# Loads of q, k and v queued behind attention's transposes, and the router's two halves side by side, in an attention, MoE, MoE kernel

## The chip, the cores and the metric

One Trainium2 chip, of which one core is used. The metric is the device time of one execution in microseconds (us). The time before is the median of three runs.

## What is computed

Causal attention with a decay, then a dense feed-forward layer with a squared ReLU ("MoE1"), then a layer of eight experts of which each token uses two ("MoE2"), all in fp32 as the reference has it:

```python
# q, k, v: (4, 8, 576, 64), f: (4, 8, 576)
cum = np.cumsum(np.log(np.clip(f, 0.0001, 1.0)), axis=-1)
scores = q @ k.T / 8 + (cum[:, :, :, None] - cum[:, :, None, :])   # causal
x = softmax(scores) @ v                        # -> (2304, 512)
h = np.maximum(x @ w_in, 0.0)                  # (2304, 2048)
x = h * h @ w_out                              # (2304, 512)
logits = x @ w_gate + np.log1p(np.exp(x @ w_noise)) * noise    # (2304, 8)
# top two experts by softmax of their logits; out = sum of gate * (relu(x @ w1[e]) @ w2[e])
```

## The kernel before

**Precision.** The matmuls run on fp16 pairs: a high part and a low remainder of each operand, and three products (high x high, high x low, low x high; the list `HL3`). So each fp32 product is three fp16 products that are summed in PSUM.

**Attention.** The four batches have 576 queries each. The first 256 of each ("head") are done in a part of their own, of 12 sub-units (`subs`); the first eight of them, and the first eight feed-forward blocks of chunk 0, follow an order written out by hand (`PLAN`, L58). The rest is 48 units `(b, i, p)`: batch, block of 128 queries (i = 2, 3, 4; the last has 64), pair of heads. A unit goes through four steps, one "tick" apart (`att_tick`, L971): scores and exponentials (`att_s`, `att_exp`), the split into high and low parts and a DMA transpose on SP's queue into `pt` (`att_split`, L280; the transposes are at L291 for i = 2, 3 and at L302 for i = 4), and, three ticks after the split, the product with the values (`att_pv`, L330 and L333). The head's last sub-units have the same transpose at L516 and the product at L529. Here such a transpose into `pt` is called a turn.

**Operands of a unit.** For each batch and pair, q and k are loaded by `load_qk` (L110, 896 KB, two buffers `qkr`), and made into high and low parts by `prep` (ScalarE L207, L208, DVE L209, L210, a small DMA L213 on POOL's queue). v is loaded by `load_v` (L104, 320 KB, two buffers `vr`) and split by `prep_v` (ScalarE L220, DVE L221). In a tick with i = 4, batch b + 1 is prepared for pair p, and the load of its next pair is written right behind that; loads of v stand in the ticks with i = 4 and i = 2.

**MoE1.** The 2304 tokens are six chunks of 384; the hidden 2048 are 16 blocks. A step of the main loop (from L1120) does the first layer of one block (`mm1`, L599, 12 matmuls of 384 columns, then ReLU and square on ScalarE, L606 to L610) and the second layer of the block two steps before (`mm2`, L655, nine matmuls of 512 columns). Chunks 0 and 1 are done in two passes each of eight blocks. The ticks of attention are spread over the steps by `target` (L1145): `until` says which tick a pass has to reach. The third pass (n = 2: chunk 0, blocks 8 to 15) has the first seven ticks. The weights of a block are loaded by `load_w` (L555, 1 MB): the first eight on SP's queue, the others on POOL's, and converted by `conv_w`.

**Router and MoE2.** When a chunk is done, `x2_out` scales it, splits it and turns it (`x2T`), and a few steps later `router` computes 8 + 8 columns of logits for its three tiles of 128 tokens (L742, 36 matmuls per chunk: three tiles, four parts of the 512, three products of 16 columns), then the top two and, in `slots`, each token's place in its experts' tables. MoE2 gathers the rows of an expert and runs its two layers (L931, L948).

**What sets the order.** Behind the hand-written part (from L1102), a scheduler orders the instructions of each engine: by their place in the program, and by when a simulated machine finds them ready. DMAs are issued in the order of the queue of the engine that issues them (SP, or POOL). `tc.issue_after(x)` orders by hand: what its block traces on the same engine as x comes behind x on that engine; instructions of other engines are not tied, and nothing waits for x to finish. The dictionary `pin` holds the instructions so used. `pin["sp"]` is set at L1088 and by the head's turns at L516, and used by `load_v` and `load_qk` (L103, L109); `pin["pool"]` is the last load of weights on POOL's queue.

Of the kernel before, what the change touches and what calls it, by code (L numbers as in the profile page):

```python
# [37 lines left out]
NT = CH // 128  # L38
# [34 lines left out]
def attn_moe_moe_kernel(ctx: ExitStack, tc, qka, qk, v, fr, w_io, wgn, noise, w1, w2, out):  # L73
# [206 lines left out]
    def att_split(u):  # L280
        b, i, p = u
        pr, = st[u]
        if i < 4:
            phl = astream.tile([128, 4, 2, 2, 128], F16, name="phl", bufs=3)
            pt = astream.tile([128, 4, 2, 2, 128], F16, name="pt", bufs=3)
            for h in range(2):
                pv = pr[:, h, :128 * (i + 1)].rearrange("p (k s) -> p k s", s=128)
                hi, lo = phl[:, :i + 1, h, 0, :], phl[:, :i + 1, h, 1, :]
                nc.scalar.activation(hi, pv, AF.Copy)  # L289
                nc.vector.tensor_tensor(lo, pv, hi, op=ALU.subtract)  # L290
            nc.sync.dma_start_transpose(out=pt[:, :i + 1].rearrange("p a b c q -> p (a b c) q"),  # L291
                                        in_=phl[:, :i + 1].rearrange("p a b c s -> p (a b c s)"))
        else:
            pt = astream.tile([128, 5, 2, 128], F16, name="pt", bufs=3)
            ph4 = astream.tile([128, 5, 2, 128], F16, name="ph4", tag="phl", bufs=3)
            nc.gpsimd.memset(ph4[:, 4, :, 64:128], 0.0)
            flat = pr.rearrange("p z s -> p (z s)")
            for k0, k1, w_ in ((0, 4, 128), (4, 5, 64)):
                s3 = flat[:, 128 * k0:128 * k0 + w_ * (k1 - k0)].rearrange("p (k s) -> p k s", s=w_)
                nc.scalar.activation(ph4[:, k0:k1, 0, :w_], s3, AF.Copy)  # L300
                nc.vector.tensor_tensor(ph4[:, k0:k1, 1, :w_], s3, ph4[:, k0:k1, 0, :w_], op=ALU.subtract)
            nc.sync.dma_start_transpose(out=pt.rearrange("p a b q -> p (a b) q"),  # L302
                                        in_=ph4.rearrange("p a b s -> p (a b s)"))
        st[u] = [pt]

    po_t = {}
# [425 lines left out]
    def router(c, pool=(psS, "S", 3, 512), behind=None):  # L732
        rt = gpool
        pl = pool[0].tile([128, pool[3]], F32, name="pl", tag=pool[1], bufs=pool[2])
        for t in range(NT):
            x = 0
            for cc in range(4):
                for wi, xi in HL3:
                    with ExitStack() as guard:
                        if behind is not None:  # L740
                            guard.enter_context(tc.issue_after(behind))
                        nc.tensor.matmul(pl[:, 16 * t:16 * t + 16], x2T_t[t][:, 4 * xi + cc, :], wg[:, cc, wi, :],  # L742
                                         start=(x == 0), stop=(x == 11))
                    x += 1
        lg = rt.tile([128, NT, 16], F32, name="lg", bufs=1)
        nc.vector.tensor_scalar(lg, pl[:, :16 * NT].rearrange("p (t e) -> p t e", t=NT), 2.0 ** -17, None, op0=ALU.mult)
        e_ = rt.tile([128, NT, NE], F32, name="e_", bufs=1)
        u_ = rt.tile([128, NT, NE], F32, name="u_", bufs=1)
        l_ = rt.tile([128, NT, NE], F32, name="l_", bufs=1)
        nc.scalar.activation(e_, lg[:, :, 8:16], AF.Exp)  # L750
        nc.vector.tensor_scalar(u_, e_, 1.0, None, op0=ALU.add)
        nc.scalar.activation(l_, u_, AF.Ln)
        d_ = rt.tile([128, NT, NE], F32, name="d_", bufs=1)
        nc.vector.tensor_scalar(d_, u_, -1.0, None, op0=ALU.add)
        nc.vector.tensor_sub(e_, e_, d_)
        nc.vector.reciprocal(u_, u_)
        nc.vector.tensor_mul(e_, e_, u_)
        nc.vector.tensor_add(l_, l_, e_)
        nc.vector.tensor_mul(l_, l_, nz[:, NT * c:NT * c + NT, :])
        nl = rt.tile([128, NT, NE], F32, name="nl", bufs=1)  # L760
        nc.vector.tensor_add(nl, l_, lg[:, :, 0:8])
        m8 = rt.tile([128, NT, 8], F32, name="m8", bufs=1)
        i8 = rt.tile([128, NT, 8], U32, name="i8", bufs=1)
        for t in range(NT):
            nc.vector.max(m8[:, t, :], nl[:, t, :])
            nc.vector.max_index(i8[:, t, :], m8[:, t, :], nl[:, t, :])
        idf = rt.tile([128, NT, 2], F32, name="idf", bufs=1)
        nc.vector.tensor_copy(idf, i8[:, :, 0:2])
        ent = rt.tile([128, NT, 2, 2], I32, name="ent", bufs=3)
        gv = ent.bitcast(F32)  # L770
        dd = rt.tile([128, NT], F32, name="dd", bufs=1)
        ed = rt.tile([128, NT], F32, name="ed", bufs=1)
        nc.vector.tensor_sub(dd, m8[:, :, 1], m8[:, :, 0])
        nc.scalar.activation(ed, dd, AF.Exp)
        nc.vector.tensor_scalar(dd, ed, 1.0, 1.0e-9, op0=ALU.add, op1=ALU.add)
        nc.vector.reciprocal(gv[:, :, 0, 1], dd)
        nc.vector.tensor_mul(gv[:, :, 1, 1], ed, gv[:, :, 0, 1])
        for t in range(NT):
            nc.vector.tensor_scalar(ent[:, t, :, 0], pid.to_broadcast([128, 2]), SPARE + CH * c + 128 * t, None, op0=ALU.add)
        oh = rt.tile([128, NT, 2, NE], F32, name="oh", bufs=1)  # L780
        for t in range(NT):
            for k in range(2):
                nc.vector.tensor_scalar(oh[:, t, k, :], iota8, idf[:, t, k:k + 1], None, op0=ALU.is_equal)
        m_ = rt.tile([128, NT, NE], F16, name="m_", bufs=1)
        nc.vector.tensor_add(m_, oh[:, :, 0, :], oh[:, :, 1, :])
        for t in range(NT):
            j = NT * c + t
            nc.vector.tensor_add(mprev[:, j + 1, :], mprev[:, j, :], m_[:, t, :])
        return m_, oh, ent
# [181 lines left out]
    def att_tick(k, pool_of):  # L971
# [12 lines left out]
        if k < NU:  # L984
# [6 lines left out]
            b, i, p = u  # L991
            if i == 4 and b + 1 < B:
                prep(b + 1, p)
                if p < 3:
                    load_qk(b + 1, p + 1)
                elif b + 2 < B:
                    load_qk(b + 2, 0)
                if p > 1:
                    load_v(b + 1, p - 2)
            if i == NB and b:  # L1000
                prep_v(b, p)
                if p < 2:
                    load_v(b, p + 2)
        if k % 4 == 1:
            x_copies(k)
        if 0 <= k - 1 < NU:
            att_split(units[k - 1])

    turn = [0]

# [109 lines left out]
    for s_i, (n, c, i) in enumerate(steps):  # L1120
# [21 lines left out]
            slots(c - 1, router(c - 1, bank), bank)  # L1142
        a0, a1 = ([-3] + until)[n] + 3, until[n] + 3
        i0, i1 = passes[n][1:]
        target = a0 + (a1 - a0) * (i - i0 + 1) // (i1 - i0)  # L1145
        j = s_i - NA + NPL
        if NPL <= j < NSUB + 3:
            hd_tick(j, main_bank)
# [15 lines left out]
        for w_i in new:  # L1164
            with tc.issue_after(pin["prev"]):
                conv_w(w_i)
            if w_i + 2 < NF:
                with tc.issue_after(pin["pool"]):
                    pin["pool"] = load_w(w_i + 2, nc.gpsimd).ins
        if c in (2, 3) and i % 4 == 3:  # L1170
            zero_out(4 * (c - 2) + i // 4)
# [169 lines left out]
```

## Time and profile before

| | us |
|---|---|
| median of 3 runs | 959.05 |
| lowest, highest | 950.98, 960.93 |
| the profiled execution, its own time | 958.06 |
| its span, first to last instruction | 956.1 |
| PE busy in the span | 929.3 |
| DVE, ScalarE (ACT), POOL busy | 567.7, 447.3, 205.1 |

The profile is of one execution. PE is TensorE's matmul, PEld its weight load, SPq the queue of SyncE, on which most DMAs are issued; times within it count from the span's start. A DMA's row in a timeline shows how long its issue took, not its transfer; the time to its landing is told apart. In brackets behind a row stand the engine's idle time ahead of it and what ended it. Matmuls overlap, so a group's span is what counts, not the sum of their durations.

### The profile page before, as it was taken

Reading aid. Unit: us, or ns where it says so; the run is one execution under the profiler, and the core shown is the slowest. Engines: PE = TensorE matmul, PEld = TensorE weight load, DVE = VectorE, ACT = ScalarE, POOL = GpSimd, SP = SyncE. Lnnn points to the kernel's source line nnn. Section 1 sums busy time; section 2 is a strip of 40 time slices with the busy share of each in tenths; the row PEclk is TensorE's granted clock in tenths of the full one; section 3 lists DMA queues with packets and bytes.
Section 4 is the critical chain, followed back from the end, with each engine's and each line's share of the span. In section 5 each row is a group of like instructions: output and inputs, shape, how many; then the busy total and the mean of one; then the engine's idle time right before and its main releaser. Section 6 shows DMA issues by size and latency. Waiting matters only on the chain.

```text
span 956.1 us, 17598 instructions
## 1 busy us (share of the span) xinstructions
PE 929.3 (97%) x6859; PEld 540.5 (57%) x6859; DVE 567.7 (59%) x1254; ACT 447.3 (47%) x990; POOL 205.1 (21%) x247
## 2 busy tenths in 40 slices
PE   9899989998999999999999999999999999999995
PEld 6675545554555555555555444656574747565652
DVE  7987968877878778776364552545261525343220
ACT  6776679866567567755343421424050504132110
POOL 5000030022121032011024135342414141211102
PEclk9899999999999999999999999999999999999998
DMA  9566799969789858936168946696968594841203
GB/s 341 172 186 193 189 283 269 165 184 199 174 187 227 192 139 204 170 57 110 29 206 218 223 115 122 146 249 181 192 147 202 141 202 114 172 98 21 35 12 44
DMA packets 220871, 155.60 MB, mean 163 GB/s; under 512 B 176690, under 2 KB 187314, under 8 KB 218738
## 3 DMA queue, kind: packets, MB, share of 16 engines
q1 hardware_dynamic: 208370, 125.14, 53.8%
q0 software_dynamic: 12416, 29.31, 15.1%
q8 instruction: 55, 0.90, 0.4%
q14 instruction: 30, 0.25, 0.1%
HBM read 89.05 MB, written 23.98 MB: 118 GB/s over the span
## 4 chain that ended last, share of the span: by engine, by line
PE 82%; DMA 7%; issue 4%; DVE 3%; ACT 2%; POOL 0%; SPq 0%; POOLq 0%; DVEq 0%; ACTq 0%
PE e L948 21%; PE e L931 20%; PE acc L655 16%; PE m L599 13%; PE m1s L599 3%; PE po L330 2%; DMA w<-in_w_io_dram 2%; DMA pt<-phl 1%; DMA qkr<-in_qk_dram 1%; PE ps L237 1%; PE po L472 1%; PE ps L238 1%; PE po L333 1%; DMA pt<-ph 1%; PE ps L248 1%
## 5 line engine op out<-in xcount | busy, mean ns | idle before, releaser
L948 PE MATMUL e<-w2s,hT 128*128 128x512 f16 (+1 forms) x960 | 209.3, 379 | 0.8 <-DVE hT L936 0.8
L655 PE MATMUL acc<-w,g 128*128 128x512 f16 x864 | 205.6, 379 | 0.0
L931 PE MATMUL e<-xgT,w1s 128*128 128x310 f16 (+2 forms) x1536 | 204.7, 294 | 0.0
L931 PEld LDWEIGHTS <-w1s 128*128 128x128 f16 x1536 | 139.6, 97 | 63.9
L599 PE MATMUL m<-xT,w 128*128 128x384 f16 x960 | 172.5, 328 | 2.1 <-ACT r L606 1.6
L935 ACT ACTIVATE hT<-e 128x310 f16<-128x310 f32 (+2 forms) x128 | 54.4, 429 | 251.7 <-PE e L931 251.4
L948 PEld LDWEIGHTS <-hT 128*128 128x128 f16 (+1 forms) x960 | 99.5, 104 | 107.4 <-DVE hT L936 1.3
L599 PEld LDWEIGHTS <-w 128*128 128x128 f16 x1152 | 108.8, 98 | 76.5 <-issue 5.3
L655 PEld LDWEIGHTS <-g 128*128 128x128 f16 x864 | 81.3, 98 | 87.5 <-issue 0.9
L951 DVE TENSOR_SCALAR y<-e,gs 128x512 f32<-128x512 f32 (+1 forms) x40 | 30.0, 750 | 151.6 <-PE e L948 141.7
L936 DVE SCALAR_TENSOR_TENSOR hT<-e,hT 128x310 f16<-128x310 f32 (+2 forms) x128 | 60.5, 477 | 65.0 <-ACT hT L935 64.8
L952 POOL DMA_INDIRECT out_dram<-y,tix x40 | 65.1, 1627 | 141.9 <-DVE y L951 135.0
L813 POOL DMA_INDIRECT table<-ent,si x36 | 42.0, 1167 | 133.8 <-DVE si L810 77.5
L889 POOL DMA_INDIRECT xg<-x2d,tix x40 | 42.4, 1059 | 125.2 <-DMA xgT<-xg 117.8
L266 DVE TENSOR_REDUCE sm<-ps 128x1 f32<-128x384 f32 (+2 forms) x96 | 52.9, 562 | 25.6 <-PE ps L239 12.3
L606 ACT ACTIVATE r<-m 128x384 f32<-128x384 f32 x80 | 39.1, 488 | 52.2 <-PE m L599 52.1
L616 DVE TENSOR_TENSOR r<-r 128x384 f32<-128x384 f32 x64 | 35.3, 552 | 35.4 <-ACT g L607 35.3
L269 ACT ACTIVATE pr<-ps,sm 128x384 f32<-128x384 f32 (+1 forms) x64 | 40.2, 630 | 30.0 <-DVE sm L268 22.5
L607 ACT ACTIVATE g<-r 128x384 f16<-128x384 f32 x96 | 50.2, 523 | 3.3 <-PE acc L655 1.3
L854 DVE SCALAR_TENSOR_TENSOR w2s<-wr,w2s 128x1024 f16<-128x1024 f32 x32 | 39.1, 1222 | 19.6 <-ACT w2s L853 19.5
L853 ACT ACTIVATE w2s<-wr 128x1024 f16<-128x1024 f32 x32 | 33.7, 1052 | 30.8 <-DMA wr<-in_w_dram 30.1
L290 DVE TENSOR_TENSOR phl<-pr,phl 128x384 f16<-128x384 f32 (+1 forms) x64 | 39.0, 619 | 12.8 <-ACT phl L289 12.3
(282 smaller groups left out, 1071.7 us busy)
## 6 DMA issues: line engine op xcount, KB each, us to landing
wr<-in_w_dram SPq DMA_DIRECT2D x64, 512.0 KB, 4.7
qkr<-in_qk_dram SPq DMA_DIRECT2D x16, 896.0 KB, 5.5
w<-in_w_io_dram SPq DMA_DIRECT2D x8, 1024.0 KB, 5.6
w<-in_w_io_dram POOLq DMA_DIRECT2D x8, 1024.0 KB, 5.5
vr<-in_v_dram SPq DMA_DIRECT2D x16, 320.0 KB, 4.0
x2d<-x SPq DMA_DIRECT2D x18, 256.0 KB, 2.7
hraw<-in_qka_dram SPq DMA_DIRECT2D x8, 512.0 KB, 8.9
out_dram<-zero SPq DMA_DIRECT2D x5, 768.0 KB, 4.2
```

The costliest lines, as they stand in the source:

```text
L266: seen[u] = nc.vector.tensor_reduce(sm[:, z:z + 1], ps[z][:, :N], AX.X, ALU.max).ins
L269: nc.scalar.activation(pr[:, z, :N], ps[z][:, :N], AF.Exp, bias=sm[:, 2 + z:3 + z], scale=SC_S, accum_out=su[:, p // 2, z, p % 2:p % 2 + 1])
L599: nc.tensor.matmul(ps, W[i][:, wi, 0, 128 * cc:128 * cc + 128], xT[:, xi, cc, r0:r0 + CH], start=(x == 0), stop=(x == 11))
L607: nc.scalar.activation(g[:, 0, :], r, AF.Square, scale=2.0 ** -10)
L655: last[0] = nc.tensor.matmul(acc[t], g[:, gi, 128 * t:128 * t + 128], W[i][:, wi, 1, :], start=(i in ends[c][0] and x == 0), stop=(i in en ...
L813: s_ = nc.gpsimd.indirect_dma_start(out=table, out_offset=bass.IndirectOffsetOnAxis(ap=si[:, t, k:k + 1], axis=0), in_=ent[:, t, k, :], in ...
L889: nc.gpsimd.indirect_dma_start(out=xg, out_offset=None, in_=x2d[0:seen, :], in_offset=bass.IndirectOffsetOnAxis(ap=rows_t[key, j][0], axis=0))
L931: last[0] = nc.tensor.matmul(ps[:, :hw], w1s[:, cc, wi, 128 * i:128 * i + 128], xgT[:, 4 * xi + cc, c], start=(x == 0), stop=(x == 11)).ins
L935: relu[0] = nc.scalar.activation(hi, ps[:, :hw], AF.Relu).ins
L936: nc.vector.scalar_tensor_tensor(hT[:, i, 1, c], ps[:, :hw], 0.0, hi, op0=ALU.max, op1=ALU.subtract)
L948: last[0] = nc.tensor.matmul(ps[:m], hT[:, i, hi, 128 * j:128 * j + m], w2s[:, i, wi, :], start=(i == 0 and x == 0), stop=(i == NFE - 1 an ...
L952: s_ = nc.gpsimd.indirect_dma_start(out=out, out_offset=bass.IndirectOffsetOnAxis(ap=ix[:m], axis=0), in_=y[:m], in_offset=None, compute_o ...
```

## The change

Four edits, in five places. (1) `att_split` stores its transpose as `pin["sp"]`, so that each later load of q, k or v is issued behind the latest turn traced before it; and in `att_tick` the loads in the ticks with i = 4 and i = 2 are traced after the tick's `att_split` and not before it. (2) The loads of MoE1's weights on POOL's queue are put under `issue_after(pin["sp"])` too. (3) The router multiplies the high part of x by the high and low parts of the weights in one matmul of 32 columns, and the low part by the high part in one of 16; the two halves of the 32 columns are added behind the matmuls by one more DVE instruction. (4) In the third pass the ticks are one step later; in the other passes `target` is as it was.

```diff
--- before.py
+++ after.py
@@ -288,8 +288,8 @@
                 hi, lo = phl[:, :i + 1, h, 0, :], phl[:, :i + 1, h, 1, :]
                 nc.scalar.activation(hi, pv, AF.Copy)
                 nc.vector.tensor_tensor(lo, pv, hi, op=ALU.subtract)
-            nc.sync.dma_start_transpose(out=pt[:, :i + 1].rearrange("p a b c q -> p (a b c) q"),
-                                        in_=phl[:, :i + 1].rearrange("p a b c s -> p (a b c s)"))
+            pin["sp"] = nc.sync.dma_start_transpose(out=pt[:, :i + 1].rearrange("p a b c q -> p (a b c) q"),
+                                                    in_=phl[:, :i + 1].rearrange("p a b c s -> p (a b c s)")).ins
         else:
             pt = astream.tile([128, 5, 2, 128], F16, name="pt", bufs=3)
             ph4 = astream.tile([128, 5, 2, 128], F16, name="ph4", tag="phl", bufs=3)
@@ -299,8 +299,8 @@
                 s3 = flat[:, 128 * k0:128 * k0 + w_ * (k1 - k0)].rearrange("p (k s) -> p k s", s=w_)
                 nc.scalar.activation(ph4[:, k0:k1, 0, :w_], s3, AF.Copy)
                 nc.vector.tensor_tensor(ph4[:, k0:k1, 1, :w_], s3, ph4[:, k0:k1, 0, :w_], op=ALU.subtract)
-            nc.sync.dma_start_transpose(out=pt.rearrange("p a b q -> p (a b) q"),
-                                        in_=ph4.rearrange("p a b s -> p (a b s)"))
+            pin["sp"] = nc.sync.dma_start_transpose(out=pt.rearrange("p a b q -> p (a b) q"),
+                                                    in_=ph4.rearrange("p a b s -> p (a b s)")).ins
         st[u] = [pt]
 
     po_t = {}
@@ -735,15 +735,19 @@
         for t in range(NT):
             x = 0
             for cc in range(4):
-                for wi, xi in HL3:
+                for xi in range(2):
+                    w_ = 32 >> xi
                     with ExitStack() as guard:
                         if behind is not None:
                             guard.enter_context(tc.issue_after(behind))
-                        nc.tensor.matmul(pl[:, 16 * t:16 * t + 16], x2T_t[t][:, 4 * xi + cc, :], wg[:, cc, wi, :],
-                                         start=(x == 0), stop=(x == 11))
+                        nc.tensor.matmul(pl[:, 32 * t:32 * t + w_], x2T_t[t][:, 4 * xi + cc, :],
+                                         wg[:, cc].rearrange("p a b -> p (a b)")[:, :w_],
+                                         start=(x == 0), stop=(x == 7), skip_group_check=True)
                     x += 1
         lg = rt.tile([128, NT, 16], F32, name="lg", bufs=1)
-        nc.vector.tensor_scalar(lg, pl[:, :16 * NT].rearrange("p (t e) -> p t e", t=NT), 2.0 ** -17, None, op0=ALU.mult)
+        p2 = pl[:, :32 * NT].rearrange("p (t a e) -> p t a e", t=NT, a=2)
+        nc.vector.tensor_scalar(lg, p2[:, :, 0, :], 2.0 ** -17, None, op0=ALU.mult)
+        nc.vector.scalar_tensor_tensor(lg, p2[:, :, 1, :], 2.0 ** -17, lg, op0=ALU.mult, op1=ALU.add)
         e_ = rt.tile([128, NT, NE], F32, name="e_", bufs=1)
         u_ = rt.tile([128, NT, NE], F32, name="u_", bufs=1)
         l_ = rt.tile([128, NT, NE], F32, name="l_", bufs=1)
@@ -991,20 +995,22 @@
             b, i, p = u
             if i == 4 and b + 1 < B:
                 prep(b + 1, p)
+            if i == NB and b:
+                prep_v(b, p)
+        if k % 4 == 1:
+            x_copies(k)
+        if 0 <= k - 1 < NU:
+            att_split(units[k - 1])
+        if k < NU:
+            if i == 4 and b + 1 < B:
                 if p < 3:
                     load_qk(b + 1, p + 1)
                 elif b + 2 < B:
                     load_qk(b + 2, 0)
                 if p > 1:
                     load_v(b + 1, p - 2)
-            if i == NB and b:
-                prep_v(b, p)
-                if p < 2:
-                    load_v(b, p + 2)
-        if k % 4 == 1:
-            x_copies(k)
-        if 0 <= k - 1 < NU:
-            att_split(units[k - 1])
+            if i == NB and b and p < 2:
+                load_v(b, p + 2)
 
     turn = [0]
 
@@ -1142,7 +1148,7 @@
             slots(c - 1, router(c - 1, bank), bank)
         a0, a1 = ([-3] + until)[n] + 3, until[n] + 3
         i0, i1 = passes[n][1:]
-        target = a0 + (a1 - a0) * (i - i0 + 1) // (i1 - i0)
+        target = a0 + (a1 - a0) * (i - i0 + (n != 2)) // (i1 - i0)
         j = s_i - NA + NPL
         if NPL <= j < NSUB + 3:
             hd_tick(j, main_bank)
@@ -1165,7 +1171,7 @@
             with tc.issue_after(pin["prev"]):
                 conv_w(w_i)
             if w_i + 2 < NF:
-                with tc.issue_after(pin["pool"]):
+                with tc.issue_after(pin["pool"]), tc.issue_after(pin["sp"]):
                     pin["pool"] = load_w(w_i + 2, nc.gpsimd).ins
         if c in (2, 3) and i % 4 == 3:
             zero_out(4 * (c - 2) + i // 4)
```

## Rows read from the trace of the kernel before

**Rows 1.** The page: busy us per engine (share, instructions), and the granted clock in 40 slices.

```profile
PE 929.3 (97%) x6859; PEld 540.5 (57%) x6859; DVE 567.7 (59%) x1254; ACT 447.3 (47%) x990; POOL 205.1 (21%) x247
...
PEclk9899999999999999999999999999999999999998
```

**Rows 2.** PE's waits over the span: who waited for what, us in total, times, longest.

```profile
PE po L333 <- DMA pt<-ph: 3.0, 1, 3.0
PE po L330 <- DMA pt<-phl: 2.1, 2, 1.2
PE po L529 <- DMA pt<-phl: 2.0, 2, 1.6
...
PE m L599 <- ACT r L606: 1.6, 4, 0.6
PE ps L237 <- DVE setk L209: 1.3, 1, 1.3
```

**Rows 3.** Timeline of PE, last chunk's router: start us, length us, line, tiles, count.

```profile
549.90 1.05 PE L742 MATMUL pl<-wg,x2T 128*128 128x16 f16 x36
550.80 5.34 PE L931 MATMUL e<-xgT,w1s 128*128 128x512 f16 x24
```

**Rows 4.** Timeline of SP's queue and PE, 157 to 166 us, around unit 1's turn.

```profile
157.99 0.57 SPq L104 DMA_DIRECT2D vr<-in_v_dram  x1
...
158.66 2.40 SPq L291 DMA_TRANSPOSE pt<-phl  x1
...
164.61 0.41 PE L330 MATMUL po<-vs,pt 128*128 128x64 f16 x8 [0.88 <-DMA pt<-phl]
```

**Rows 5.** Tile `pl`, its reader: duration ns min/median/max, first and last start.

```profile
L746 DVE TENSOR_SCALAR lg<-pl x6: 198/204/208, 197.1 to 551.3; 128x48 f32<-128x48 f32 x6
```

**Rows 6.** Timeline of SP's queue, 209 to 216 us.

```profile
210.38 0.33 SPq L110 DMA_DIRECT2D qkr<-in_qk_dram  x1
211.28 2.88 SPq L104 DMA_DIRECT2D vr<-in_v_dram  x2
214.58 2.75 SPq L302 DMA_TRANSPOSE pt<-ph  x1
```

**Rows 7.** Timeline of PE at 223 us, the product that needs that turn.

```profile
223.12 0.66 PE L333 MATMUL po<-vs,pt 128*64 128x64 f16 x30 [3.03 <-DMA pt<-ph]
```

**Rows 8.** Tile `pt`, its DMAs: time from issue to landing.

```profile
DMA to landing us min/median/max: 3.4/4.4/8.0
```

**Rows 9.** Stretch 223.9 to 227.3 us: PE, PEld, DVE, ACT, POOL busy, clock, DMA.

```profile
223.90:227.30 3.40, 3.40 (x12) 1.66 (x11) 0.82 (x1) 2.26 (x5) 0.00 (x0) 0.50 0.99 279
```

**Rows 10.** Timeline of SP's queue, 256 to 273 us.

```profile
261.81 0.53 SPq L727 DMA_DIRECT2D out_dram<-zero  x1
263.77 9.57 SPq L291 DMA_TRANSPOSE pt<-phl  x3
```

**Rows 11.** Timeline, 111 to 115 us: a weight load on POOL's queue, a head's turn.

```profile
111.74 0.53 POOL L555 DMA_DIRECT2D w<-in_w_io_dram  x1 [7.65 <-DVE w L579]
...
114.09 3.38 SPq L516 DMA_TRANSPOSE pt<-phl  x1
```

**Rows 12.** Timeline, 132 to 136 us: first preparation of k, first scores.

```profile
132.44 1.16 ACT L207 ACTIVATE setk<-qkr 128x1152 f16<-128x1152 f32 x1 [4.06 <-DMA qkr<-in_qk_dram]
...
135.11 0.49 PE L237 MATMUL ps<-setk,setq 128*128 128x384 f16 x2 [1.34 <-DVE setk L209]
```

**Rows 13.** Tile `qkr`, its DMAs: time from issue to landing.

```profile
DMA to landing us min/median/max: 4.8/5.5/7.7
```

**Rows 14.** Timeline of SP's queue and ACT's L207, near 190 and near 360 us.

```profile
189.10 3.47 SPq L291 DMA_TRANSPOSE pt<-phl  x1
...
191.51 1.16 ACT L207 ACTIVATE setk<-qkr 128x1152 f16<-128x1152 f32 x1
...
358.69 0.93 SPq L110 DMA_DIRECT2D qkr<-in_qk_dram  x1
...
360.74 1.15 ACT L207 ACTIVATE setk<-qkr 128x1152 f16<-128x1152 f32 x1
```

## The prediction

> **What bounds the kernel now.** I read the page's first two parts, then the list of what TensorE (PE) waited for, then the timeline around each wait that a load or a turn could have caused. "Turn" means the DMA transpose from `phl` or `ph` into `pt`, which carries one attention unit's softmax to the values' matmuls. The first rows are to be read together: PE is busy 929.3 of 956.1 us, and the clock row is at 9 in nearly every slice [rows 1]. So the kernel is bound by PE's own work, and another order of loads can give back only PE's idle time, 26.8 us with its start and its end, and what the clock lost.
>
> The waits tell how much is within reach [rows 2]. Three groups wait for a turn: `po` L333 (3.0 us, once), `po` L330 (2.1 us, twice) and `po` L529 (2.0 us, twice). One group waits for DVE's preparation of k and q (`ps` L237, 1.3 us), and the first layer's matmul waits for ScalarE four times (1.6 us together). No other wait that this change could touch is longer than 0.8 us. These five groups come to 10.0 us, about 1% of the time.
>
> **The router's matmuls.** Per chunk, 36 products of 16 columns become 12 of 32 and 12 of 16 columns: 12 fewer matmuls and weight loads, 72 fewer in six chunks. The last chunk's 36 start at 549.90 us and the next layer's matmuls at 550.80 us [rows 3], so 0.90 / 36 = 25 ns each. No row has a 32-column matmul. If it costs what a 16-column one does, the gain is 72 x 25 ns = 1.8 us. From the other side, eight matmuls of 64 columns took 0.41 us with the end of the last [rows 4], at most 51 ns each; at that price a chunk's new sum is 12 x 25 + 12 x 51 = 912 ns, the old 0.90 us, and the gain is nothing. I take 1.8 us, since 32 is nearer to 16. The Trainium skill (TensorE: Matmul & The Clock Gate, Wait — 56ns, not 53.3ns?) names the same 25 ns as a floor and says that 32 columns are on it; by that the 1.8 us would stand.
>
> The two halves must now be summed by one more DVE instruction per chunk. The read of the sums that is there took 204 ns [rows 5], so six more cost 1.2 us of DVE. Nothing at best, 1.2 us if PE waited each time; I take nothing: behind it come only the router's small DVE work and the table, and PE has first- and second-layer matmuls to do meanwhile; its list of waits names no DVE result of the router. Without that cover it would be the 1.2 us.
>
> **Loads of q, k and v behind the turns.** The pin `sp` was set last in the head's part, so it held a load behind a turn long done; loads went into SP's queue as soon as their buffer was free. Now the pin moves with every turn, and the loads of a tick are traced after its turn. Nothing is added: the same 16 + 16 DMAs, in another place of SP's queue; the turns, `xT`, `x2T` and `x2d` transfers beside them keep their order.
>
> The largest wait shows what this is worth. SP issued a load of `qkr` (896 KB) at 210.38 us and two of `vr` (320 KB each) from 211.28 us, and only then, at 214.58 us, the turn of unit 10 [rows 6]. PE needed that turn and stood for 3.03 us, until 223.12 us [rows 7], which is 8.5 us after the issue; the median turn lands 4.4 us after it [rows 8]. At the median it would have landed at 219.0 us, before PE asked for it (223.12 - 3.03 = 220.09 us). All three loads (q and k of batch 2, pair 0; v of batch 1, pairs 2 and 3) are traced in ticks 11 to 13 and go, by the new pin, behind turn 10. So 3.0 us go. The clock then fell: from 223.9 to 227.3 us half the clock (1.2 of 2.4 GHz) was granted, with PE busy all along [rows 9]; 3.4 us at half speed did 1.7 us of work, so 1.7 us go too if the wait was its cause. Its cause is not certain (nothing to 1.7 us); I take 1.7, as PE had just stood. Together 4.7 us.
>
> The next turn wait of this sort is at 164.61 us: a `vr` load issued at 157.99 us, the turn at 158.66 us, PE 0.88 us idle [rows 4]. That load (v of pair 3) is now tied behind this very turn; the v load one tick earlier comes between the two turns instead, and the load of batch 1's second q, k pair leaves this stretch altogether. So one `vr` still runs ahead of the turn, but with one load fewer around it: nothing to 0.9 us, and I take 0.9.
>
> Two turn waits stay: that of L529 (below), and the second of L330. This one, 1.2 us long [rows 2], is that of the turn queued at 263.77 us, two microseconds behind a store of zeros [rows 10], which isn't touched. What could change it is only another order of everything before it.
>
> **Loads of MoE1 weights.** The new pin is on SP's instruction, while the load is issued on POOL's queue, and the helper ties only instructions of the named one's own engine. So this edit orders nothing. The wait of L529 has such a load 2.35 us ahead of its turn (111.74 and 114.09 us [rows 11]) and stays. Nothing, then; if the pin did hold, 2.0 us would be the gain and, at worst, one conversion of weights would be late by the length of a turn's issue.
>
> **The first attention tick one step later.** All ticks of the third pass move by one step; the next pass's first step, which had none, takes the seventh. At 132.44 us ScalarE had stood 4.06 us for the first q, k load, and PE then 1.34 us for the scores [rows 12]. A step has nine second-layer matmuls of 512 columns; 24 matmuls of that width took 5.34 us [rows 3], so nine alone are 2.0 us, more than the 1.34. The scores then come after the preparation, and the 1.3 us go (nothing, if the preparation moves with them). The step's matmuls are only moved. ScalarE's waits there (four, 1.6 us [rows 2]) may move either way by as much; I take nothing.
>
> **What the later loads cost.** Before, q and k came long ahead of their preparation; now the load of pair p+1 goes behind a turn of the tick before the one that prepares it. A load lands 5.5 us after its issue [rows 13]. Turn 7's issue ran from 189.10 for 3.47 us, to 192.57 us; the load behind it lands at 198.1 us, but its preparation on ScalarE began at 191.51 us: 6.6 us late [rows 14]. In the third batch the place behind the turn is at 358.69 us, the landing 364.2 us, the preparation 360.74 us: 3.4 us late [rows 14]. The other ticks lie far enough apart. Nothing if ScalarE has other work to put first, and 10 us if PE pays every microsecond. ScalarE's 4.06 us of waiting cost PE 1.34 us [rows 12]; I take one such wait, 1.3 us.
>
> **The sum.** -1.8 - 4.7 - 0.9 - 1.3 + 1.3 = -7.4 us, from the profiled execution's 958.1 us (its span of 956.1 us and 2.0 us around it) to 950.7 us. The median of the three runs is 1.0 us above that execution, so the forecast for a median is 951.7 us.
>
> **Rivals.** (1) *Loads too late.* The Trainium skill (DMA: Bandwidth & Descriptors, Rules for kernel authors) advises the opposite of this edit: issue a DMA early, wait for it late. That the first scores stood for a load which ScalarE awaited agrees with it; that these loads come too late no run here shows yet. As a mechanism of this kernel: ScalarE works in order, so a preparation that stands for its load holds the next `r` and `g`, and PE the next first-layer matmul. Price: 6.6 + 3.4 = 10.0 us and one drop of the clock like the one seen, 1.7 us, in place of my 1.3: 951.7 + 10.4 = 962.1 us, slower than before. It decides where a tick is shorter than turn plus landing, as at 191.51 us; against it, 1.34 of 4.06 us reached PE the one time that it was seen. (2) *The turns stay as late.* A load behind one turn is ahead of the next, and the same bytes move. Then only the router and the first tick are left, 1.8 + 1.3: 956.9 us. For it: in the stretch from 189 us, ticks are so close that loads and turns alternate already. Against it: the one long wait had three loads in front, of which none is left. (3) *More goes than I count.* The MoE1 pin holds after all or the order clears the rest (2.0 + 1.2 us), and ScalarE's late load costs nothing (1.3): 951.7 - 4.5 = 947.2 us. For it: all turns of 8 us stand behind a bulk transfer.
>
> **How the numbers follow.** Forecast 0.52, late loads 0.13, turns as late 0.18, more goes 0.17. The range reaches from just below the third rival, 945 us, to 961 us, near the first. About 1%, 9.6 us, is what a measurement of this kernel can tell from no change; that is 949.5 and 968.6 us. Below 949.5 us lie the third rival and a third of the forecast's own spread: 0.34. Above 968.6 us is only a first rival with several drops of the clock: 0.08. The rest, 0.58, is within.
>
> **What would show it.** Right: no wait of PE near 220 us for a turn and no half clock behind it, no wait for `setk` at the first scores, 144 router matmuls 25 ns apart, SP's `qkr` and `vr` rows each behind a turn, POOL's weight loads where they were. Wrong: ScalarE waiting for `qkr` in the stretch of the fifth blocks, with PE behind it, or the turns still landing 8 us after their issue.

## The result, and the profile after

The changed kernel is slower: 965.69 us against 954.05 us, both medians of 11 runs on the same chip, ratio 1.0107 (95% interval 1.0079 to 1.0136; the ratio is not the quotient of the two medians, which is 1.0122). I had forecast 951.7 us and a range up to 961 us. The profiled execution took 963.22 us; that of before, 958.06 us. So the two traces differ by 5.2 us, less than the medians do: the profiled execution of before lay above the median of its 11 runs, that of after below its own. Of all the executions in this document one, of the kernel with the loads as early as their buffers allow, took 1073.71 us at a mean clock of 0.847, and its ratio leaves that one out.

The page of the changed kernel, the rows that answer to [rows 1]:

```profile
PE 926.8 (96%) x6787; PEld 538.9 (56%) x6787; DVE 568.7 (59%) x1260; ACT 446.3 (46%) x990; POOL 206.0 (21%) x247
...
PEclk9799999999999999999999999999999999999999
```

PE has 2.5 us less to do and takes 5.4 us more of span. So PE stands more, and the list of its waits says for whom. This is the changed kernel's, answering to [rows 2]:

```profile
PE m L599 <- ACT r L606: 8.7, 7, 2.9
PE ps L237 <- ACT pr L276: 3.6, 1, 3.6
PE ps L237 <- ACT pr L269: 3.1, 1, 3.1
...
PE ps L248 <- ACT pr L276: 0.9, 1, 0.9
```

The waits of `po` L330 and L333 for a turn are gone, all 5.1 us of them. In their place PE waits for ScalarE, 16.3 us in these four groups where it was 1.6 us. What did ScalarE wait for? Its own list, from 130 to 480 us, first of the changed kernel, then of the one before:

```profile
ACT setk L207 <- DMA qkr<-in_qk_dram: 18.4, 7, 4.3
...
ACT vs L220 <- DMA vr<-in_v_dram: 11.9, 6, 6.3
```

```profile
ACT setk L207 <- DMA qkr<-in_qk_dram: 5.3, 3, 4.1
```

Before, ScalarE never waited for v, and for q and k only at the start of attention. Now it stands some 30 us for loads, 4.1 us of them at the first preparation as before (4.06 us [rows 12]). How such a wait reaches PE is seen best at 190 us, in the changed kernel's timeline of SP's queue, ACT and PE (start us, length us, line, tiles, count):

```profile
189.27 3.19 SPq L291 DMA_TRANSPOSE pt<-phl  x1
...
192.51 0.63 SPq L110 DMA_DIRECT2D qkr<-in_qk_dram  x1
...
198.60 1.16 ACT L207 ACTIVATE setk<-qkr 128x1152 f16<-128x1152 f32 x1 [4.32 <-DMA qkr<-in_qk_dram]
...
200.44 0.47 ACT L606 ACTIVATE r<-m 128x384 f32<-128x384 f32 x1
...
200.97 1.30 PE L599 MATMUL m<-xT,w 128*128 128x384 f16 x7 [2.90 <-ACT r L606]
```

Read it downward. Turn 7 is issued until 192.46 us and the load behind it at 192.51 us, as the edit wants. ScalarE is idle for 4.32 us ahead of L207, the preparation of this very pair. Behind L207 in ScalarE's order stands L606, which empties the one PSUM buffer of the first layer (`m`), and PE needs that buffer for its next twelve matmuls: 2.90 us of PE. In the kernel before the same pair had been loaded some 40 us earlier.

The longest wait is v's, at 229 us:

```profile
218.60 1.32 SPq L302 DMA_TRANSPOSE pt<-ph  x1
219.98 0.69 SPq L110 DMA_DIRECT2D qkr<-in_qk_dram  x1
220.71 0.44 SPq L104 DMA_DIRECT2D vr<-in_v_dram  x1
...
230.56 0.74 ACT L220 ACTIVATE vs<-vr 128x640 f16<-128x640 f32 x1 [6.25 <-DMA vr<-in_v_dram]
...
232.34 0.32 PE L237 MATMUL ps<-setk,setq 128*128 128x384 f16 x1 [3.61 <-ACT pr L276]
```

Behind turn 10 both loads of the tick are queued, q and k first; `vr` lands near 230.5 us, 9.8 us after its issue, and ScalarE stands for 6.25 us. The exponentials that are to empty the scores' buffers (L276) are behind it, and PE waits 3.61 us for a buffer. The clock fell behind it as it had before [rows 9]; the stretch's columns are as there:

```profile
233.40:236.80 3.40, 3.26 (x11) 1.53 (x11) 2.92 (x10) 1.80 (x5) 0.00 (x0) 0.50 0.64 123
```

The sum over the two profiled executions: router -1.8 us; turn waits of L330 and L333 -5.3 us (0.13, 0.88, 3.03 and 1.24 us before); five waits of PE behind ScalarE's waits for loads +12.7 us (at 198, 229, 299, 310 and 372 us: 2.90, 3.61, 0.85, 3.10, 2.23 us); one wait at 669 us -0.8 us. That is +4.8 of the 5.2 us. The lost clock is the same in these two executions: 10.2 us at half speed within the first 40 us, 3.4 us behind one long wait, and the end of the span.

That is not so of all executions. The mean granted clock of the changed kernel's 11 executions is 0.9876 (0.984 to 0.992); that of the kernel before, in the three other series of runs below, is 0.9909 to 0.9912. An estimate from these: 0.0034 x 965 us, some 3 us of the loss that the two traces do not show. One of the kernels below (preparation traced a tick later) has the changed kernel's order of instructions on every engine and shows it in its trace. PE stands at the same five places for 12.2 us (3.51, 1.91, 0.86, 3.03 and 2.86 us), and behind four of them half the clock was granted for 3.4 us each; the columns are those of [rows 9]:

```profile
200.70:204.10 3.40, 3.40 (x20) 1.70 (x19) 2.92 (x15) 1.75 (x5) 0.86 (x2) 0.50 0.88 88
231.40:234.80 3.40, 3.40 (x13) 1.64 (x12) 2.92 (x9) 2.33 (x7) 0.00 (x0) 0.50 0.47 91
313.30:316.70 3.40, 3.40 (x27) 1.55 (x25) 2.97 (x8) 3.02 (x9) 0.00 (x0) 0.50 0.86 195
374.80:378.20 3.40, 2.98 (x10) 1.46 (x10) 2.88 (x8) 1.92 (x3) 1.10 (x2) 0.51 0.13 48
```

Four times 1.7 us is 6.8 us, where the changed kernel's profiled execution lost 1.7 us. Which of the waits a fall of the clock follows differs from one execution to the next: the wait of 3.10 us near 310 us had none behind it, the same wait of 3.03 us in the other execution had one.

### The profile page after: what moved, and what is told of

Same layout as the page of the kernel before. It is cut to its first block, busy times and chain, and to the rows that moved or that the text cites. A ratio compares the mean times of both kernels' runs of the same rounds, so it can differ in the third digit from the quotient of the medians.

```text
span 961.5 us, 17435 instructions
## 1 busy us (share of the span) xinstructions
PE 926.8 (96%) x6787; PEld 538.9 (56%) x6787; DVE 568.7 (59%) x1260; ACT 446.3 (46%) x990; POOL 206.0 (21%) x247
## 4 chain that ended last, share of the span: by engine, by line
PE 68%; DMA 3%; ACT 1%; SPq 1%; issue 1%; POOL 0%; DVE 0%; ACTq 0%; POOLq 0%; DVEq 0%
PE e L935 21%; PE e L952 21%; PE acc L655 10%; PE m L599 8%; PE m1s L599 3%; DMA qkr<-in_qk_dram 2%; PE po L330 1%; PE ps L237 1%; PE ps L238 1%; PE po L333 1%; DMA vr<-in_v_dram 1%; PE ps L248 0%; DMA x2T<-x 0%; SPq L302 0%; POOL out_dram L956 0%
## 5 line engine op out<-in xcount | busy, mean ns | idle before, releaser
L655 PE MATMUL acc<-w,g 128*128 128x512 f16 x864 | 205.2, 379 | 0.0
L599 PE MATMUL m<-xT,w 128*128 128x384 f16 x960 | 172.0, 328 | 9.4 <-ACT r L606 8.7
L599 PEld LDWEIGHTS <-w 128*128 128x128 f16 x1152 | 109.1, 98 | 85.1 <-issue 13.8
L655 PEld LDWEIGHTS <-g 128*128 128x128 f16 x864 | 81.2, 98 | 87.0 <-ACT g L607 0.5
L606 ACT ACTIVATE r<-m 128x384 f32<-128x384 f32 x80 | 38.7, 484 | 44.7 <-PE m L599 44.3
L290 DVE TENSOR_TENSOR phl<-pr,phl 128x384 f16<-128x384 f32 (+1 forms) x64 | 40.1, 635 | 14.4 <-ACT phl L289 14.1
L858 DVE SCALAR_TENSOR_TENSOR w1s<-wr,w1s 128x1024 f16<-128x1024 f32 x32 | 38.8, 1227 | 11.4 <-ACT w1s L857 11.0
```

The costliest lines, as they stand in the source:

```text
L599: nc.tensor.matmul(ps, W[i][:, wi, 0, 128 * cc:128 * cc + 128], xT[:, xi, cc, r0:r0 + CH], start=(x == 0), stop=(x == 11))
L655: last[0] = nc.tensor.matmul(acc[t], g[:, gi, 128 * t:128 * t + 128], W[i][:, wi, 1, :], start=(i in ends[c][0] and x == 0), stop=(i in en ...
L858: nc.vector.scalar_tensor_tensor(lo, t_, sc, hi, op0=ALU.mult, op1=ALU.subtract)
```

## The experiments

Every kernel was timed beside the kernel before on the same chip, in four series: the changed kernel; the three parts alone; the four kernels with v, with q and k, one tick's turn earlier, and as early as buffers allow; the other four. A ratio holds within its series. The median of before was 954.05, 959.25, 953.61 and 953.24 us in the four, the second and the third on one chip and 0.6% apart, so ratios of different series compare only roughly. Theory A: the loads come too late behind the turns, and ScalarE passes that on to PE. Theory B: another order of the engines, brought by the router or the later tick, is the loss. Theory C came up on the way: an edit can change the scheduler's order as a whole, and that moves the time by some us.

| kernel | median us | ratio to before | 95% interval |
|---|---|---|---|
| changed | 965.69 | 1.0107 | 1.0079 to 1.0136 |
| router alone | 950.46 | 0.9881 | 0.9843 to 0.9918 |
| later tick alone | 960.29 | 0.9999 | 0.9971 to 1.0028 |
| loads alone | 976.73 | 1.0171 | 1.0128 to 1.0214 |
| changed, v as before | 957.55 | 1.0031 | 1.0000 to 1.0063 |
| changed, q and k as before | 951.31 | 0.9968 | 0.9944 to 0.9993 |
| changed, loads one tick's turn earlier | 956.01 | 1.0022 | 0.9990 to 1.0053 |
| changed, loads as early as buffers allow | 956.68 | 1.0021 | 0.9992 to 1.0051 |
| router and later tick | 949.30 | 0.9959 | 0.9936 to 0.9982 |
| neutral edit of the router | 956.21 | 1.0037 | 1.0010 to 1.0065 |
| changed, preparation traced a tick later | 965.81 | 1.0129 | 1.0099 to 1.0160 |
| the same, held back on ScalarE | 962.00 | 1.0116 | 1.0086 to 1.0146 |

### Each part alone

**The router's edit in the kernel before** (the diff's hunk of `router`, nothing else).

> The kernel before with the router's edit alone. Both theories: the router costs 1.8 us less of PE (72 matmuls of 25 ns), so about 952 us where before is 954. Theory A (late loads are the whole loss): no new wait of ScalarE for qkr or vr, ratio 0.995 to 1.002. Theory B (another order of the engines, brought by fewer matmuls or by the later tick, is the loss): 5 us or more above before, ratio over 1.005, with PE waiting where the changed kernel waits.

Ratio 0.9881: more than the 1.8 us, and faster than either theory allowed. The part that I had worked out is right to the row: the last chunk's 24 matmuls, half of 32 and half of 16 columns, here in the changed kernel's timeline of PE, take 0.60 us from their start to the next layer's, 25 ns each as before ([rows 3]).

```profile
556.83 0.75 PE L743 MATMUL pl<-wg,x2T 128*128 128x32 f16 x24
557.43 5.34 PE L935 MATMUL e<-xgT,w1s 128*128 128x512 f16 x24
```

The rest came from elsewhere. This kernel has the loads as the kernel before has them, and yet SP's queue stands in another order. The timeline of SP's queue, router alone, and PE's wait for the second turn:

```profile
208.60 0.33 SPq L110 DMA_DIRECT2D qkr<-in_qk_dram  x1
209.78 0.38 SPq L104 DMA_DIRECT2D vr<-in_v_dram  x1
210.63 2.84 SPq L302 DMA_TRANSPOSE pt<-ph  x1
213.57 0.53 SPq L110 DMA_DIRECT2D qkr<-in_qk_dram  x1
214.80 0.47 SPq L104 DMA_DIRECT2D vr<-in_v_dram  x1
217.18 3.31 SPq L302 DMA_TRANSPOSE pt<-ph  x1
...
225.20 0.41 PE L333 MATMUL po<-vs,pt 128*64 128x64 f16 x14 [1.30 <-DMA pt<-ph]
```

Compare [rows 6]: there both `vr` loads were ahead of the turn of unit 10; here one of them is behind it. The wait for the turn of unit 10 (3.03 us) is gone, unit 11's is 1.30 us, and neither is followed by half the clock. So 3.4 of the 4.7 us that I had put down to the loads' edit (3.03 - 1.30, and the 1.7 us of clock) were to be had without it.

**The later tick in the kernel before.**

```diff
-        target = a0 + (a1 - a0) * (i - i0 + 1) // (i1 - i0)
+        target = a0 + (a1 - a0) * (i - i0 + (n != 2)) // (i1 - i0)
```

> The kernel before with the first attention tick one step later alone. My prediction said 1.3 us less (no wait for setk at the first scores). In the changed kernel that wait became one of 1.4 us of the first layer's matmul for ScalarE, so Theory A: the same time as before within 2 us, the 1.3 us wait only renamed. Theory B: 5 us or more above before.

Ratio 0.9999: nothing. The changed kernel's timeline shows why, against [rows 12]:

```profile
133.46 1.16 ACT L207 ACTIVATE setk<-qkr 128x1152 f16<-128x1152 f32 x1 [4.11 <-DMA qkr<-in_qk_dram]
...
135.68 0.47 ACT L606 ACTIVATE r<-m 128x384 f32<-128x384 f32 x1
136.19 0.97 PE L599 MATMUL m<-xT,w 128*128 128x384 f16 x5 [1.42 <-ACT r L606]
```

The scores no longer wait for `setk`, but ScalarE stands for the same load as long as before, and the step that was to cover the gap needs its buffer `m` emptied by L606, which stands behind the preparation. The wait is renamed from `ps` L237 to `m` L599, 1.34 to 1.42 us. In the trace of the tick alone it is the same, 1.50 us of L599 at 135.0 us. That trace has other waits than before, too: 0.83 us for a turn at 221 us where there were 3.03, but 2.50 us of L330 at 345 us, with 3.4 us at half the clock behind it.

**The loads' edit in the kernel before** (all other hunks of the diff).

> The kernel before with the order of the loads alone (pin and place, and the pin on the weight loads). Theory A: all of the loss is here: ScalarE stands for qkr and vr together 25 to 30 us (before: some 5), PE waits behind it some 10 to 13 us, waits for turns L330 and L333 are gone; time some 966 us where before is 954, ratio 1.009 to 1.015. Theory B: ratio under 1.004.

Ratio 1.0171: of the three parts, this one alone costs time, and somewhat more than theory A's range of 1.009 to 1.015. Theory B falls. ScalarE's waits for loads from 130 to 480 us are 35.7 us, above the 25 to 30 expected:

```profile
ACT vs L220 <- DMA vr<-in_v_dram: 16.3, 8, 6.5
ACT setk L207 <- DMA qkr<-in_qk_dram: 12.0, 4, 6.7
ACT setq L208 <- DMA qkr<-in_qk_dram: 7.4, 3, 3.7
```

A third expectation was missed: waits for turns are not gone in this kernel. PE's list still has them, larger than before:

```profile
PE m L599 <- ACT r L606: 8.1, 7, 3.0
PE po L330 <- DMA pt<-phl: 4.4, 3, 2.1
PE po L333 <- DMA pt<-ph: 2.5, 1, 2.5
```

SP's queue stood 104.6 us for the splits that its turns carry (L290, L301) where it was 65.4 us before. So the turns themselves came later; that they did because ScalarE's share of the split was late fits, but is argued.

**The weight loads' pin.** Without it the changed kernel's program is the same, instruction for instruction: it orders nothing, as forecast.

### v or q and k

**v as before, q and k behind the turns**: the changed kernel with a pin of its own for `load_v`, which stays at the head's last turn, and its two calls back at their old places.

```diff
-        with tc.issue_after(pin["sp"]):
+        with tc.issue_after(pin["head"]):
             nc.sync.dma_start(t, v[b, :, 128 * p:128 * p + 128].rearrange("(k s) d -> s k d", s=128))
...
```

> The changed kernel with the loads of v back where they were and pinned as they were; only q and k stay behind the turns. If the late v loads are one part of the loss and the late q, k loads the other: the waits of PE behind ScalarE at 229 and 310 us (3.6 and 3.1 us in the changed kernel, both begun by prep_v's wait for vr) go, those at 198, 299 and 372 us (2.9, 0.9, 2.2 us, begun by prep's wait for qkr) stay: some 957 to 960 us. If q, k alone are the loss: 964 to 966 us. If v alone is: 950 to 953 us.

957.55 us, within the first case. ScalarE's waits for v are gone, those for q and k are 17.8 us:

```profile
ACT setk L207 <- DMA qkr<-in_qk_dram: 10.4, 5, 4.8
ACT setq L208 <- DMA qkr<-in_qk_dram: 7.4, 2, 5.5
```

Of PE's waits behind q and k, that at 198 us stands (3.42 us, half the clock behind it); those at 299 and 372 us do not, and at 364 us there is one of 2.61 us (`acc` L655).

**q and k as before, v behind the turns** (the same with `load_qk`).

> The changed kernel with the loads of q and k back where they were and pinned as they were; only v stays behind the turns. Both late: the waits of PE behind ScalarE for qkr (6.0 us together) go, those for vr (6.7 us and a drop of the clock) stay: 957 to 960 us. q, k alone the loss: 950 to 953 us. v alone the loss: 964 to 966 us.

951.31 us: below the first case and within the second. What is left of ScalarE's waits:

```profile
ACT vs L220 <- DMA vr<-in_v_dram: 5.9, 3, 3.1
ACT setk L207 <- DMA qkr<-in_qk_dram: 4.0, 2, 3.9
ACT setq L208 <- DMA qkr<-in_qk_dram: 2.6, 2, 1.5
```

So the parts don't add up. Against the kernel with router and tick but all loads as before (0.9959, below; another series), v behind the turns costs 0.1%, which is nothing that these intervals tell from none, q and k behind them 0.7%, both together 1.5%. The longest wait of the changed kernel fits with this: v's load had q's and k's queued ahead of it. With q and k back at their places, ScalarE's waits for v are half as long, 5.9 us for 11.9.

### How late

**Loads traced ahead of the tick's split**, at their old place, with the new pin: each is behind the turn of the tick before.

```diff
             if i == 4 and b + 1 < B:
                 prep(b + 1, p)
+                if p < 3:
+                    load_qk(b + 1, p + 1)
+                elif b + 2 < B:
+                    load_qk(b + 2, 0)
+                if p > 1:
+                    load_v(b + 1, p - 2)
...
```

> The changed kernel with the loads traced where they were, ahead of the tick's att_split; the pin moves with the turns, so each load is tied behind the turn of the tick before. If the lateness of one tick is the loss: ScalarE's waits for qkr and vr fall from 30 us to under 12, PE's waits behind it from 13 us to under 5, time 950 to 956 us. If being behind any turn is the loss, whichever it is: 960 us or more.

956.01 us: 1.5% of loss against all loads as before became 0.6%, just past the first case's end. ScalarE's waits for loads from 130 to 480 us are 17.2 us where under 12 were expected; none is for v:

```profile
ACT setk L207 <- DMA qkr<-in_qk_dram: 8.9, 3, 4.9
ACT setq L208 <- DMA qkr<-in_qk_dram: 8.3, 4, 3.8
```

**Loads as early as their buffers allow, still behind a turn.**

```diff
+        if k == 1:
+            load_qk(1, 1)
...
-                if p < 3:
-                    load_qk(b + 1, p + 1)
+                if p < 2:
+                    load_qk(b + 1, p + 2)
                 elif b + 2 < B:
-                    load_qk(b + 2, 0)
-                if p > 1:
-                    load_v(b + 1, p - 2)
+                    load_qk(b + 2, p - 2)
+            if i == 3 and b + 1 < B and p > 1:
+                load_v(b + 1, p - 2)
```

> The changed kernel with each load of q and k behind a turn but one tick earlier (pair p + 2 in the tick that prepares pair p, as soon as its buffer is free), and the loads of the next batch's first two v pairs at i = 3 in place of i = 4. Theory A (late loads are the loss, turns first are a gain): ScalarE's waits for qkr and vr under 8 us, no wait of PE for a turn over 1 us, time 945 to 952 us, below both kernels. If a load must be in front of the turns to be in time: 955 us or more, with turn waits or waits for qkr still there.

956.68 us: a miss for my hope that this would beat both kernels, and in the second case by its time. ScalarE still waited 20.5 us from 130 to 480 us. A place behind a turn is more than a place in the program: SP issues in order, and a turn first waits for DVE's split, so whatever is behind it waits too. In this kernel these waits of SP's queue are 73.3 us, in the changed kernel 99.1 us, in the kernel before 65.4 us. The changed kernel's, then those of the kernel before:

```profile
SPq L291 <- DVE phl L290: 56.5, 18, 8.1
...
SPq L302 <- DVE ph L301: 42.6, 12, 10.5
```

```profile
SPq L291 <- DVE phl L290: 41.9, 18, 8.5
...
SPq L302 <- DVE ph L301: 23.5, 12, 5.2
```

**The preparation a tick later, loads as in the change.**

```diff
-            if i == 4 and b + 1 < B:
-                prep(b + 1, p)
+            if k and units[k - 1][1] == 4 and units[k - 1][0] + 1 < B:
+                prep(units[k - 1][0] + 1, units[k - 1][2])
```

> The changed kernel with the preparation of q, k traced one tick later and the loads where the change has them. If a tick too few between load and preparation is the cause: ScalarE's waits for qkr behind 190 us (15 us in the changed kernel) fall under 5 us, 955 to 960 us. If the scheduler puts the preparation where its own simulated load has landed, whichever tick it is traced in, and the chip's load lands later than that: the order of ScalarE stays nearly the same, the waits stay over 10 us, 962 to 968 us.

965.81 us, ratio 1.0129, the second case. The order of all five engines is that of the changed kernel, row for row: where the scheduler puts the preparation does not follow from the tick in which it is traced. So this run repeats the changed kernel, and its trace is the second one of that order (the four falls of the clock above). That the preparation stands where the scheduler's own simulated load has landed, sooner than the chip's, fits with this and with ScalarE's waits; no row shows the simulated landings, so it remains argued.

**The same, with the preparation tied on ScalarE behind the tick's last exponential.**

```diff
...
+                with tc.issue_after(pin["exp"]):
+                    prep(units[k - 1][0] + 1, units[k - 1][2])
```

> The same, with the preparation also queued behind the exponentials of the tick in which it is traced, so that the scheduler can't take it forward. Late loads of q, k: ScalarE's waits for qkr behind 190 us fall under 3 us, PE's waits behind them at 198, 299 and 372 us (6.0 us) go, the waits for vr (12 us of ScalarE) stay: 956 to 961 us. If the time doesn't follow ScalarE's waits for qkr: 964 us or more.

962.00 us, between the two cases. ScalarE's waits for q and k fell as expected (3.8 us, once, at the start), those for v fell to 7.6 us where they were to stay at 12, and PE waits for `r` only 2.5 us. But the loads are issued as late as ever, and what comes behind the preparation is late now: the small DMA that lays the decay's rows into `setk`, for which PE's list has

```profile
PE ps L238 <- DMA setk<-c: 5.0, 3, 2.5
...
PE po L333 <- DMA pt<-ph: 2.4, 2, 1.9
```

Around two of these waits, which ended at 220 us (1.94 us, L333) and 222 us (2.06 us, L238), half the clock was granted for 6.8 us. So the lateness was moved, at least in part, from ScalarE's order to the chain load, preparation, decay rows, scores. How much of the 962.00 us this is stays open: the profiled execution, of 957.70 us, was the fastest of the six.

### What the order alone does

**Router and later tick, all loads as before.**

> The kernel before with the router and the later tick, all loads as before. If the loads are the whole loss of the changed kernel: as the router alone, ratio 0.985 to 0.995, no ScalarE wait for vr, 1 us or less for qkr behind 150 us. If the later tick harms beside the router: ratio 1.0 or more.

949.30 us, ratio 0.9959: below both kernels, though just above the expected 0.985 to 0.995, with one wait of ScalarE for `qkr` of 2.9 us at 277 us that was not expected. It is the changed kernel without its loads' edit, so that edit costs (1.0107 / 0.9959) 1.5%, some 14 us, with the router's edit in place, and 1.7% without it. Within one series, the kernel with the changed kernel's order took 965.81 us where this one took 949.30: 1.7%. PE's list, with no wait for ScalarE over 1.4 us:

```profile
PE m L599 <- ACT r L606: 4.1, 5, 1.4
...
PE po L333 <- DMA pt<-ph: 1.1, 1, 1.1
```

**A neutral edit**: the logits read by two DVE instructions of half the width, all 36 matmuls kept.

```diff
-        nc.vector.tensor_scalar(lg, pl[:, :16 * NT].rearrange("p (t e) -> p t e", t=NT), 2.0 ** -17, None, op0=ALU.mult)
+        p2 = pl[:, :16 * NT].rearrange("p (t e) -> p t e", t=NT)
+        nc.vector.tensor_scalar(lg[:, :, 8:16], p2[:, :, 8:16], 2.0 ** -17, None, op0=ALU.mult)
+        nc.vector.tensor_scalar(lg[:, :, 0:8], p2[:, :, 0:8], 2.0 ** -17, None, op0=ALU.mult)
```

> The kernel before with the router's logits read out of PSUM by two DVE instructions of half the width in place of one; the 36 matmuls per chunk stay. It adds some 1 us of DVE in all and takes nothing from PE. Theory C (the router's edit gained 1.8 us by its matmuls and some 7 us by the other order that the scheduler then chose): this kernel, whose order also changes, moves by several us as well, to either side, and its wait of PE for the turn near 220 us is another. Rival D (the gain is the matmuls' or that of sums taken side by side): ratio 0.997 to 1.003.

Ratio 1.0037 (1.0010 to 1.0065): some 3.5 us for 0.9 us more of DVE (reads of 176 and 172 ns in place of one of 204 ns, six times), which no wait of PE names. Of the 305 DMAs that SP issues, 22 are other ones than before at their place in the queue, with the router's edit 31. PE's wait for the turn near 220 us is 2.05 us where it was 3.03, without half the clock behind it. So an edit of next to no weight moved the time by about half of the 7.4 us that I had summed, as theory C has it; but the interval reaches down into rival D's range, and one edit of this sort is not a measure of how far the order moves the time. How much of the router's gain is order, and how much its own, stays open: beside the 1.8 us it was 7 us by the medians of one series (0.9881) and, with the tick that alone does nothing, 2 us in another (0.9959).

## Why the prediction was wrong, point by point

- **The step that failed is "What the later loads cost".** Its mechanism was right, and so was the first place (a preparation 6.6 us late near 191 us [rows 14]; ScalarE stood 4.3 us there). Its size was not: I took one wait of PE of 1.3 us; it measured 12.7 us, in five places, and in a second execution of the same order 12.2 us with 6.8 us of clock behind it. Most of the miss is the count. I found 10.0 us of lateness in two places and wrote that the other ticks lie far enough apart; ScalarE stood 26.8 us behind the first preparation, in 13 waits. I priced q and k alone: v was late as well, by up to 6.25 us of ScalarE. And even of my 10.0 us I took only what one wait had cost: the row's own scale, 4.06 us of ScalarE for 1.34 us of PE [rows 12], gives 3.3 us for 10.0 and 8.8 us for 26.8. That scale was too low, but less so: in that row PE had second-layer matmuls to do meanwhile; at 198 us 4.32 us cost 2.90, at 229 us 6.25 us cost 3.61, and 26.8 us in all cost 12.7, nearly a half and not a third.
- **The other failed step is "The first attention tick one step later".** Its 1.3 us was counted as gone; it was renamed. The step that was to cover the wait stands behind the same ScalarE. The four waits of 1.6 us [rows 2] that were left out of the sum as ScalarE's are PE's for ScalarE.
- **Turn waits: right in the trace, wrong in what it was worth.** The waits at 164 and 223 us went, and that at 272 us, which I had left in place. But the long one was an accident of that order: with the router's edit alone it is gone too, and 1.30 us at the next turn and no fall of the clock are in its place. Counting 4.7 us for it was counting the trace of one order against another order. And a fall of the clock came back, behind a wait for ScalarE.
- **Router: right.** 144 matmuls, 25 ns apart; 1.8 us. That the sums' second DVE instruction costs PE nothing was right; its length was 204 ns.
- **Pin on the weight loads: right.** It orders nothing.
- **Rivals.** The first came true: slower, by ScalarE, close to the price of 10.0 us and a drop of the clock that I had given it (11.7 us; the trace shows 12.7 and 1.7, the second execution of the same order 12.2 and 6.8). That the price came so close is in part luck: it let PE pay all of 10.0 us, where PE paid a half of 26.8. It had a chance of 0.13. The rule that it was weighed with (the Trainium skill, DMA: Bandwidth & Descriptors, Rules for kernel authors: issue early, wait late) was the better guide than my one row, and these runs now show it, with router and tick in all three: 0.9959 with loads as before, 1.0022 with loads behind the turn of a tick before, 1.0107 behind the tick's own (three series). The second rival's 956.9 us was summed wrongly: 959.05 - 1.8 - 1.3 is 956.0 us.
- **The chances.** I gave slower by over 1% only 0.08, since the first rival had to beat the gains of the other parts first. Those gains were summed as if certain. The forecast also stood on a median of three runs, 959.05 us; eleven give 954.05.

## What to carry to other kernels

A load moved behind something in an in-order queue comes later by what that something waits for, not only by its transfer: before it is moved, find the consumer, its place in its engine's order, and what stands behind the consumer for the engine that sets the time. One idle stretch in a trace that a scheduler made is a fact of that order; a small edit can make another order (the neutral one did, the preparation traced a tick later did not), so a gain summed from single waits is worth little until neutral edits have shown how far the time moves by itself. Of a bundle of edits, run each alone: here one cost more than all the others gained.

## What had not been expected

A read of the logits in two halves, 0.9 us more of DVE in all, moved the kernel by some 3.5 us (1.0037, 1.0010 to 1.0065), and the router's edit moved it by more than its 1.8 us in both kernels that have it without the loads' edit. The `vr` load of 320 KB took 9.8 us to land where the median had been 4.0 us, with 896 KB queued ahead of it and two transposes and two stores behind it. Two executions of one order of instructions lost 1.7 and 6.8 us of clock behind PE's waits for ScalarE.
